# Attention and a dense mixture of experts on one core: padding TensorE's program early, joining local scores, re-cutting the last product

## The chip, the core and the metric
One core of one Trainium2 chip. Five engines run their own programs side by side: TensorE (PE: matrix products; its weight loads are listed as PEld), VectorE (DVE), ScalarE (ACT), GpSimd (POOL) and SyncE (SP, which here only asks for transfers). 16 DMA engines move data between main memory and the on-chip memory SBUF. Matrix products land in PSUM, a small memory of eight banks. The metric is the device time of one execution in microseconds (us), lower is better.

## The reference
```python
# q, k, v: 4 batches x 8 heads x 576 positions x 64, float32
scores = q @ k.T / 8
# heads 0..3 ("local"): position i sees j with 0 <= i - j < 32
# heads 4..7 ("strided"): i sees j <= i with i % 32 == j % 32
attn = exp(scores - max); attn = attn / (sum + 1e-9)
x = (attn @ v), heads side by side        # 2304 tokens x 512
p = probs / (probs.sum(-1) + 1e-9)        # 2304 x 4
out = sum over 4 experts e of p[:, e] * (relu(x @ w1[e]) @ w2[e])
# w1: 512 x 1024, w2: 1024 x 512
```

## The kernel before
**Work and tiles.** Attention is computed in 16 pairs (n = 0..15: a batch and a quarter of its heads, two heads of one kind), even n local (L), odd n strided (S). A pair's scores are many small products into PSUM banks of the pool "sc" (L616 for a strided pair, L627 for a local pair; a local pair's nine tiles go in two groups, gi = 0 with six and gi = 1 with three). VectorE masks them into `pmL`/`pmS` (L641) and takes the maximum, the sum and the quotient; PE transposes them (L706, L722, L739), and multiplies by the values `vstL`, `vstS` (L791 for early local pairs, L771). The result, x, is split into a rounded part `xh` (ACT, L849) and the rest `xl` (DVE, L852).

**Experts.** The first 384 tokens (of batch 0, whose four pairs are the first four) go through the experts in ordinary products of three passes (high x high, high x low, low x high): L969 for the first layer, L985 for the second. Its four chunks need the x of one pair each. The other 1920 tokens run in two parts of 896 and 1024 with a scheme of seven products per block step (`product`, L1155); there an operand is either a weight block reloaded into `a`, `s` (L1180), or a block from a ring of five buffers (`ring`, L1395), both brought by SP from main memory. A part has eight units, a unit 14 steps of 12 products or so.

**Order.** Nothing is ordered by hand. Each operation is given to a planner (class `Plan`) with an engine, a duration, the names that it reads and writes, a priority and the PSUM banks that it takes. Operations are numbered as they are added, and the table `SHIFT` moves single numbers' priorities. The planner walks a model of time and writes each engine's program. PSUM pools are "mo" (4 banks), "sc" (2) and "ps" (2). Into gaps that it foresees on PE in the first part it puts dummies (L1526): products of a tile `wz` of zeros, 128x512, whose result nobody reads.

**Engine queues.** Each engine runs its program in order, so that what stands behind a waiting instruction waits too, SP's transfers among them.

**Names.** `raw` are weights as loaded (L874), which ACT (L884) and DVE or POOL (L885) split into a high and a low part in `a`, `s`, `w2t` or `ring`. `normalize` (L1462) turns the expert probabilities into `pr`. At the end, the last product of the last unit is made in two column halves, each followed by an add (L1338) and a store (L1340).

Of the kernel before, what the change touches and what calls it, by code (L numbers as in the profile page):

```python
# [18 lines left out]
ZN = 30  # L19
# [10 lines left out]

SHIFT = {
# [5 lines left out]
}  # L37


# [4 lines left out]
class Plan:  # L44
# [14 lines left out]
    DEEPER = 5.0  # L59
    ROW = 1.0  # L60
    SWITCH = 0.17
    FIRST = 9
    SWING = 5.09
    ENGINES = ("PE", "ACT", "DVE", "POOL", "SP")
    FLEX = {"VP": ("DVE", "POOL"), "AD": ("ACT", "DVE")}
# [76 lines left out]
    def walk(self):  # L142
# [32 lines left out]
        def fill(f, s, o):  # L175

            n = 0
            while True:
                k = int(f / self.TICK + 1e-9)
                need = self.BUSY - seen.get(k, 0)  # L180
                rate = 1.0 if warm(f) else 0.5
                step = 0.2133 / rate
                if need <= 0:
                    nk = (k + 1) * self.TICK
                    if nk + step < s:
                        f = nk
                        continue
                    return n, f
                rem = (k + 1) * self.TICK - f
                forced = f > 3.4 and need / 2400 / rate <= rem and (  # L190
                    need - o.cols) / 2400 / rate > rem - max(s - f, 0.0) - o.dur / rate
                if f + step > s and not forced or not out and n >= self.FIRST:
                    return n, f
                f = stream(f, 0.2133, 512)
                n += 1
# [6 lines left out]
        def when(o):  # L202
            t = o.ready
            if o.xfer is not None and o.start is None:
                t = max(t, wire - (self.DEEP if wire < 200 else self.DEEPER))
            for i, key in enumerate(o.bank):
                n = len(allocs[key[0]]) - self.banks[key[0]] + i
                if n >= 0:
                    for p in self.readers.get(allocs[key[0]][n], ()):
                        if p.start is None:  # L210
                            return None
                        t = max(t, p.end + self.SYNC)
            return t
# [81 lines left out]
        while left:  # L295
# [29 lines left out]
            if e == "PE":  # L325
                f = free["PE"]
                if o.moe:
                    credit = min(credit + o.dur, 8.0)
                    began = True
                else:  # L330
                    credit = max(credit - o.dur * self.mix, -8.0)
                row = 0.0 if o.moe else row + o.dur
                if abs(credit) > self.swing:
                    turn = credit < 0
                if row > self.ROW:
                    turn = True
                if s < STEADY:
                    f = max(f, 1.07)
                    tag = next((t for t in allocs if not (o.bank and o.bank[0][0] == t) and clear(t, f) and not (began and t == "mo")), None)
                    n, f2 = fill(f, s, o) if tag else (0, f)  # L340
                    if n:
                        out.append((f, -1, n, tag))
                        allocs[tag].append(("idle",))
                        s = max(s, f2)
# [46 lines left out]
def attn_moe_kernel(  # L391
# [51 lines left out]
    psums = const.tile([P, NTT], F32, name="psums")  # L443
    wz = const.tile([P, 512], BF16, name="wz")
    warm = const.tile([P, 8], F32, name="warm")

    wt = {n: big.tile([P, 2, 2, 256], F32R, name=n) for n in QUART[:3] + ("s3",)}
    wq = {n: (t[:, 0], t[:, 1]) for n, t in wt.items()}
# [41 lines left out]
    KORD = (0, 2, 1, 3)  # L490
    JOIN = 4
    WHOLE = (1,)
    order = [(b, c) for b in range(B) for c in KORD]
    NP = len(order)
    plan = Plan(BANKS, MIX, tc)
# [44 lines left out]
    def plan_pair(n):  # L540
# [56 lines left out]
        for gi, (g0, g1) in enumerate(GRP[kd]):  # L597
            z = zg[gi]
            ng = g1 - g0
            key = ("sc", n, "b", gi)  # L600
            nel = ng * W

            keys = [key]
# [5 lines left out]
            def scores(keys=keys, gi=gi, g0=g0, g1=g1, v0=0):  # L609
                ss = [bank(x) for x in keys]  # L610
                if kd == "S":
                    for o in range(0, 6 * W, W):
                        for x in range(2):
                            for h in range(2):
                                a = slice(64 * h, 64 * h + 64)
                                nc.tensor.matmul(  # L616
                                    ss[h][64 * x:64 * x + 64, o:o + W], qkv[a, x, o:o + 64],
                                    qkv[a, x, QKS + o:QKS + o + SR], start=True, stop=True)
                    return
                for r in range(3):  # L620
                    for v, s in enumerate(ss, v0):
                        for h in range(2):
                            for i in range(2):
                                a = slice(64 * h, 64 * h + 64)
                                t = QB * (2 * gi + v) + (96 * i + 32 * r if spans else 64 * r + 32 * i)
                                p = 64 * (h ^ v) + 32 * i
                                nc.tensor.matmul(  # L627
                                    s[p:p + 32, r * W:r * W + W], qkv[a, t:t + 32],
                                    qkv[a, t + 193:t + 193 + W], start=True, stop=True)
# [33 lines left out]
            dd = nel / 960 + 0.15  # L663
            vp = (dd, nel * 1.6e-3 + 0.22)
            if kd == "S" and gi == 0:
                add("PE", 0.88, scores, [f"qkS{bf}{i}" for i in range(2)], keys + [f"pmS{bf}{i}" for i in range(2)], z + 3, keys,
                    cols=4 * nel)
            elif n == 0 and gi == 0:
                for i, x in enumerate(keys):
                    add("PE", 0.46, half_scores(scores, x, i), [f"qkL{bf}0" + "ab"[i]], [x, tok], z + 3, x, cols=2 * nel)  # L670
            elif kd == "L":
                add("PE", (0.68, 0.46)[gi], scores, [f"qkL{bf}{gi}"], keys + [tok], z + 3, keys, cols=4 * nel)
            for i, x in enumerate(keys if kd == "L" else [key]):
# [102 lines left out]
        for gi in range(2):  # L776
# [65 lines left out]
            for (t0, nt, nm) in ((0, TA, "x"), (T0[1], TBS[0], "r1"), (T0[2], TBS[1], "r2")):  # L842
                for sel, cols in cut(t0, nt):
# [3 lines left out]
                    if nm == "x":  # L847
# [5 lines left out]
                                out=cols(xl[c]), in0=src(), in1=cols(xh[c].bitcast(F32)), op=ALU.subtract)  # L853

                        add("ACT", 0.42, xhi, [key], [f"xh{c}{g}"], z + 7.2)
                        add("DVE", 0.44, xlo, [key, f"xh{c}{g}"], [f"xl{c}{g}"], z + 7.4)
                    else:
                        def xraw(e, src=src, cols=cols, nm=nm):
                            if e == "ACT":
# [454 lines left out]
    def plan_o(part, u, step, slot, group, last, z, due):  # L1314
# [10 lines left out]
        for f in range(2):  # L1325
# [6 lines left out]
            o0 = t0 + c * TH  # L1332
            orow = slice((2 * r + f) * P, (2 * r + f) * P + P)
            if last and step == "a22" and f == 1:
                for x in range(2):
                    cs = slice(x * TH // 2, (x + 1) * TH // 2)
                    add("PE", 0.72, lambda cs=cs, key=key: product(lhs(), rhs(), 1, key, first_in, TH, cs), need, [f"{key}{x}"], zz, None, True, 3 * TH)
                    add("DVE", 0.42, lambda i=i, cs=cs, key=key: nc.vector.tensor_tensor(  # L1338
                        out=acc[i][:, cs], in0=held[key][:, cs], in1=acc[i][:, cs], op=ALU.add), [f"{key}{x}", f"acc{i}0"], [f"end{x}"], zd)
                    add("SP", 0.4, lambda i=i, cs=cs, x=x, orow=orow, o0=o0: nc.sync.dma_start(  # L1340
                        out=out_t[orow, o0 + x * TH // 2:o0 + (x + 1) * TH // 2], in_=acc[i][:, cs]),
                        [f"end{x}"], [f"out{i}{x}"], zz + dz, xfer=((0.5, 128),))
                continue
            add("PE", dz, lambda f=f, key=key: product(lhs(), rhs(), f, key, first_in, TH),
# [116 lines left out]

    def normalize():  # L1462
        nc.vector.tensor_reduce(out=psums, in_=prs, op=ALU.add, axis=AX.X)
        nc.vector.tensor_scalar_add(out=psums, in0=psums, scalar1=1e-9)
        nc.vector.reciprocal(out=psums, in_=psums)
        nc.vector.tensor_tensor(
            out=pr, in0=prs, in1=psums.unsqueeze(2).to_broadcast([P, NTT, E]), op=ALU.mult)
# [5 lines left out]
        if n == 1:  # L1473
            add("POOL", 0.1, lambda: nc.gpsimd.memset(raws[2][:, 0, 0:1], 0.0), ["pmS00"], ["raw20", "raw21"], 0)
    add("SP", 0.4, load_pr, (), ["prs"], 8, xfer=((0.1, 128),))
    add("DVE", 1.0, normalize, ["prs"], ["pr"], ZN)
    key = ("ps", "pr")

    def turn_pr():
# [47 lines left out]

    with tc.manual_schedule():
        nc.vector.memset(wz, 0.0)
        make_identity(nc, ident)  # L1530
        for t in pm["S"]:
            nc.gpsimd.memset(t[:, :, SR + 1:64], 0.0)
            nc.gpsimd.memset(t[:, :, SR:SR + 1], 1e-9)
        for t in pm["L"]:
            nc.gpsimd.memset(t, 0.0)
            a = t[:, 0:1]
            nc.gpsimd.memset(bass.AP(a.tensor, a.offset, [list(a.ap[0]), [3 * P, 3], [P + 32, 3], [1, 1]]), 1e-9)
        plan.run(idle)
# [81 lines left out]
```

## Time and profile before

| what | value |
|---|---|
| median of 3 runs | 778.45 us (776.25, 778.45, 778.79) |
| profiled execution | 778.49 us, its span 776.7 |
| granted TensorE clock, mean | 0.998 |
| PE, DVE, ACT, POOL busy | 99%, 80%, 50%, 27% |
| first second-layer product (L985) | starts at 39.23 |
| last PE matmul ends | about 772.8 |

The span runs from the first to the last instruction; 1.8 us of the execution lie outside it. A time within the profile is counted from the start of the span. A matmul of 32-bit floats that the program writes once is shown as two instructions in rows of the trace (x24 in the program's order is x48 there). The granted clock is a share of the full 2.4 GHz; 0.5 is the lower level, 1.2 GHz.

### The profile page before, as it was taken

The page shows a single profiled execution, that of the slowest core. Times are in us where ns is not written, and L with a number is a line of the kernel's source. Part 1 is how long each engine was busy: PE and PEld are TensorE (multiplying, and loading weights), DVE is VectorE, ACT ScalarE, POOL GpSimd, SP SyncE. Part 2 cuts the span into 40 slices and gives each one's busy share as a digit, 9 for nine tenths or more (in the row PEclk, how much of TensorE's full clock was granted, in tenths as well). Part 3 has the DMA queues.
Part 4 walks back from the last instruction along what each step waited for, and adds up shares of the span by engine and source line. Part 5 has one row for each costly group of instructions (what it writes and reads, how often), then busy time and mean ns, then how long its engine had stood idle before and what let it go on. Part 6 is the DMA issues. An engine that isn't in the chain of part 4 may idle for free.

```text
span 776.7 us, 14119 instructions
## 1 busy us (share of the span) xinstructions
PE 765.5 (99%) x5374; PEld 664.6 (86%) x5377; DVE 620.8 (80%) x1016; ACT 385.6 (50%) x726; POOL 206.4 (27%) x198
## 2 busy tenths in 40 slices
PE   7999999999999999999999999999999999999997
PEld 4788888889989999999999998888888888888886
DVE  6877777798698897889798997758765976599895
ACT  4635544474566375646727654644354344523330
POOL 5412011012131522454373264001000330033250
PEclk9999999999999999999999999999999999999999
DMA  9999999778899798899989838955665697659624
GB/s 321 305 394 380 339 326 353 276 252 327 311 388 343 257 359 288 328 237 350 350 254 275 272 119 221 395 207 220 236 265 198 193 215 288 232 173 247 215 82 162
DMA packets 89630, 212.67 MB, mean 274 GB/s; under 512 B 7071, under 2 KB 33883, under 8 KB 89563
## 3 DMA queue, kind: packets, MB, share of 16 engines
q1 hardware_dynamic: 83659, 201.96, 71.8%
q0 software_dynamic: 5760, 9.70, 7.9%
q8 instruction: 42, 0.69, 0.3%
q10 hardware_dynamic: 144, 0.11, 0.1%
q14 instruction: 25, 0.20, 0.1%
HBM read 138.58 MB, written 73.17 MB: 273 GB/s over the span
## 4 chain that ended last, share of the span: by engine, by line
PE 95%; DVE 2%; DMA 1%; ACT 1%; issue 1%; POOL 0%; DVEq 0%; ACTq 0%
PE mo L1155 26%; PE ps L1155 25%; PE sc L1155 20%; PE mo L985 9%; PE mo L969 9%; PE ps L771 2%; DMA ring<-d27a 1%; PE sc L627 1%; PE ps L739 1%; PE sc L616 1%; PE mo L1526 1%; PE ps L791 0%; ACT q L1207 0%; DVE w2t L885 0%; DVE pmL L641 0%
## 5 line engine op out<-in xcount | busy, mean ns | idle before, releaser
L1155 PE MATMUL sc<-T,ring 128*128 128x448 f32 (+2 forms) x774 | 174.3, 374 | 0.0
L1155 PEld LDWEIGHTS sc<-T,ring 128*128 128x128 f32 x774 | 144.5, 188 | 19.7
L1240 ACT ACTIVATE T<-q 128x512 fp32r<-128x512 f32 (+1 forms) x196 | 112.6, 601 | 69.0 <-PE mo L1155 26.4
L1242 DVE TENSOR_TENSOR T<-q,T 128x512 fp32r<-128x512 f32 (+1 forms) x152 | 104.7, 703 | 15.9 <-ACT T L1240 15.2
L1203 DVE TENSOR_TENSOR q<-ps,v 128x448 f32<-128x448 f32 (+1 forms) x96 | 62.5, 654 | 35.3 <-PE ps L1155 30.9
L1155 PE MATMUL mo<-T,ring 128*128 128x512 f32 (+1 forms) x396 | 90.0, 376 | 0.0
L1207 ACT ACTIVATE q<-q 128x448 f32<-128x448 f32 (+1 forms) x84 | 49.9, 598 | 71.7 <-DVE q L1203 70.8
L1155 PEld LDWEIGHTS mo<-T,ring 128*128 128x128 f32 x396 | 74.3, 188 | 10.3
L1242 POOL TENSOR_TENSOR T<-q,T 128x448 fp32r<-128x448 f32 (+1 forms) x44 | 53.1, 1215 | 91.8 <-ACT T L1240 69.9
L985 PE MATMUL mo<-w2t,hs 128*128 128x512 f32 x288 | 71.2, 397 | 0.0
L1194 ACT ACTIVATE v<-mo 128x448 f32<-128x448 f32 (+1 forms) x96 | 54.5, 567 | 25.7 <-PE mo L1155 25.0
L1352 DVE TENSOR_TENSOR acc<-sc,acc 128x512 f32<-128x512 f32 (+1 forms) x85 | 54.9, 654 | 13.9 <-PE sc L1155 13.1
L1284 POOL TENSOR_TENSOR q<-q,q 128x512 f32<-128x512 f32 (+1 forms) x12 | 15.4, 1284 | 181.5 <-DVE T L1242 164.9
L985 PEld LDWEIGHTS mo<-w2t,hs 128*128 128x128 f32 x288 | 52.7, 188 | 11.0
L1284 DVE TENSOR_TENSOR q<-q,q 128x448 f32<-128x448 f32 (+1 forms) x88 | 58.9, 681 | 2.5 <-POOL T L1242 1.4
L526 ACT ACTIVATE acc<-sc 128x448 f32<-128x448 f32 (+1 forms) x41 | 23.2, 567 | 48.5 <-PE sc L1155 46.9
L969 PE MATMUL mo<-xh,a 128*128 128x384 f32 x192 | 45.7, 341 | 0.0
L1352 DVE TENSOR_TENSOR acc<-mo,acc 128x512 f32<-128x512 f32 (+1 forms) x52 | 34.0, 658 | 14.0 <-PE mo L1155 11.3
L1155 PE MATMUL ps<-T,ring 128*128 128x448 f32 (+1 forms) x180 | 40.8, 375 | 0.5 <-DMA ring<-d27a 0.5
L1155 PEld LDWEIGHTS ps<-T,ring 128*128 128x128 f32 x180 | 33.7, 188 | 5.3 <-DVE acc L1352 0.8
L1155 PE MATMUL ps<-t4h,a 128*128 128x448 f32 (+1 forms) x128 | 35.2, 376 | 0.2 <-DVE q L1203 0.2
L1155 PE MATMUL ps<-t3h,s 128*128 128x448 f32 (+1 forms) x128 | 35.2, 376 | 0.1
(179 smaller groups left out, 1437.6 us busy)
## 6 DMA issues: line engine op xcount, KB each, us to landing
raw<-in_w SPq DMA_DIRECT2D x28, 1024.0 KB, 8.3
qkS<-in_qk_strided SPq DMA_DIRECT2D x16, 329.0 KB, 8.2
vstL<-in_v_local SPq DMA_DIRECT2D x6, 640.0 KB, 9.7
po<-acc POOLq DMA_DIRECT2D x16, 224.0 KB, 7.2
vstS<-in_v_strided SPq DMA_DIRECT2D x8, 384.0 KB, 7.8
a<-d16a SPq DMA_DIRECT2D x6, 512.0 KB, 8.7
ring<-d27a SPq DMA_DIRECT2D x6, 512.0 KB, 6.5
a<-d10a SPq DMA_DIRECT2D x6, 512.0 KB, 4.7
```

The source lines that it names most:

```text
L526: nc.scalar.activation(out=dst(), in_=src(held[key]), func=AF.Copy)
L771: nc.tensor.matmul(oo[hf][64 * h:64 * h + 64, o:o + w], a, pt[r, x, c0:c0 + w], start=True, stop=True)
L969: nc.tensor.matmul(pt[:, 0:TA], w[:, c % 2, (f % 2) * P:(f % 2) * P + P], (xl if i == 1 else xh)[c], start=j == 0, stop=j == 11)
L985: nc.tensor.matmul(pt, ht[f][:, ts], wt[f][:, cs], start=j == 0, stop=j == 11)
L1155: nc.tensor.matmul(pt, a[i == 2][:, j, f * P:f * P + P], skewed(b[i == 1][j], TH)[:, cs], start=bool(first) and n == 0, stop=True, skip_gr ...
L1194: add("ACT", TH / 1200 + 0.18, lambda: nc.scalar.activation(out=late["u"][i][:, 0:TH], in_=held[key][:, 0:TH], func=AF.Copy), [key, "late2 ...
L1203: add("DVE", DD, lambda: nc.vector.tensor_tensor(out=q(), in0=src(), in1=late["u"][i][:, 0:TH], op=ALU.add), [key, f"u{i}", "late2"], [tok ...
L1207: add("ACT", TH / 1200 + 0.2, lambda: nc.scalar.activation(out=q(), in_=q(), func=AF.Relu), ["late2"], [tok], zs)
L1240: add("ACT", TH / 1200 + 0.17, lambda src=src, hi=hi: nc.scalar.activation(out=hi(), in_=src(), func=AF.Copy), [tok, "late2"], [f"T{i}h{j} ...
L1242: add("VP", vp, lambda e, src=src, hi=hi, lo=lo: engine(e).tensor_tensor(out=lo(), in0=src(), in1=hi().bitcast(F32), op=ALU.subtract), [to ...
L1284: add("VP", vp, lambda e, d=d, x=x, y=y: engine(e).tensor_tensor(out=d[0](), in0=x[0](), in1=y[0](), op=ALU.subtract), [x[1], y[1]], [d[1] ...
L1352: add("DVE", DD, lambda av=av, key=key: nc.vector.tensor_tensor(out=av(), in0=held[key][:, 0:TH], in1=av(), op=ALU.add), [key], tok, zd)
```

## The change
- The dummies ahead of PE's first operation are at most six (`FIRST`), not nine, counted until PE has run its first operation; foreseen gaps of up to 0.3 us (`SHORT`) get no dummies.
- Behind pair 1's scores stand twelve products of 128x64 zeros (`PAD`).
- From pair 4 on (`JOIN`) a local pair's scores are one operation, and its second group of three tiles takes a bank of "mo" instead of "sc". The count of banks in `when` is corrected for an operation that takes banks of two pools.
- `SHIFT` has new values, and the entries 814 to 842 are gone.
- The last product and its add and store are cut at 384 and 128 columns, not at 256 and 256.
- `normalize` adds 1e-9 from a tile `tiny` with a tensor_tensor; the planner's durations for it and for `xl` differ.

```diff
-    92: -3.6, 95: -12.5, 96: -7.9, 100: -3.6, 101: -23.3, 110: 14, 116: -12.2, 121: -23.9, 122: -23.9, 123: -42.2,
-    153: -19.6, 246: 21.6, 253: 14.6, 256: 14.6, 257: 14.6, 258: 14.6, 259: 14.6, 260: 14.6, 261: 14.6, 343: -7.1,
-    347: 2.4, 348: 6.9, 350: 17.1, 352: -6.9, 354: -22.2, 356: -12.9, 364: -31.5, 365: -12.6, 814: 2.4, 815: 6.9,
-    817: 17.1, 825: -22.2, 828: -6.9, 830: -12.9, 841: -31.5, 842: -12.6,
+    92: -3.6, 95: -12.5, 96: -7.9, 100: -3.6, 101: -23.3, 110: 14, 116: -12.2, 118: 5, 121: -23.9, 122: -23.9, 123: -42.2,
+    153: -19.6, 246: 21.6, 253: 14.6, 256: 14.6, 257: 14.6, 258: 14.6, 259: 14.6, 260: 14.6, 261: 14.6, 343: -7.1, 347: 2.4,
+    348: 6.9, 350: 17.1, 352: -6.9, 354: -22.2, 356: -12.9, 364: -31.5, 365: -12.6, 686: 7.8, 698: -5.2,
...
-    FIRST = 9
+    FIRST = 6
+    SHORT = 0.3
...
-                if f + step > s and not forced or not out and n >= self.FIRST:
+                if f + step > s and not forced or last["PE"] is None and n >= self.FIRST:
...
-                n = len(allocs[key[0]]) - self.banks[key[0]] + i
+                n = len(allocs[key[0]]) - self.banks[key[0]] + sum(x[0] == key[0] for x in o.bank[:i])
...
-                    n, f2 = fill(f, s, o) if tag else (0, f)
+                    n, f2 = fill(f, s, o) if tag and s - f > self.SHORT else (0, f)
...
+    tiny = const.tile([P, NTT], F32, name="tiny")
...
+    PAD = 12
...
-            key = ("sc", n, "b", gi)
+            whole = kd == "L" and n >= JOIN
+            key = ("mo" if whole and gi else "sc", n, "b", gi)
...
+                    for _ in range(PAD if n == 1 else 0):
+                        nc.tensor.matmul(ss[0][:, 6 * W:6 * W + 64], wz[:, 0:P], wz[:, 0:64], start=True, stop=True)
...
-                add("PE", 0.88, scores, [f"qkS{bf}{i}" for i in range(2)], keys + [f"pmS{bf}{i}" for i in range(2)], z + 3, keys,
-                    cols=4 * nel)
+                add("PE", 0.88 + (PAD * 0.03 if n == 1 else 0), scores, [f"qkS{bf}{i}" for i in range(2)], keys + [f"pmS{bf}{i}" for i in range(2)], z + 3, keys,
+                    cols=4 * nel + (PAD * 64 if n == 1 else 0))
             elif n == 0 and gi == 0:
                 for i, x in enumerate(keys):
                     add("PE", 0.46, half_scores(scores, x, i), [f"qkL{bf}0" + "ab"[i]], [x, tok], z + 3, x, cols=2 * nel)
+            elif whole:
+                if gi:
+                    plan.number += 1
+                else:
+                    k3 = keys + [("mo", n, "b", 1)]
+                    add("PE", 1.14, lambda scores=scores, k3=k3: (scores(), scores(k3[2:], 1)), [f"qkL{bf}{i}" for i in range(2)],
+                        k3 + [f"pmL{bf}{i}" for i in range(2)], z + 3, k3, cols=4 * 9 * W)
...
-                        add("DVE", 0.44, xlo, [key, f"xh{c}{g}"], [f"xl{c}{g}"], z + 7.4)
+                        add("DVE", 0.54, xlo, [key, f"xh{c}{g}"], [f"xl{c}{g}"], z + 7.4)
...
-                for x in range(2):
-                    cs = slice(x * TH // 2, (x + 1) * TH // 2)
-                    add("PE", 0.72, lambda cs=cs, key=key: product(lhs(), rhs(), 1, key, first_in, TH, cs), need, [f"{key}{x}"], zz, None, True, 3 * TH)
-                    add("DVE", 0.42, lambda i=i, cs=cs, key=key: nc.vector.tensor_tensor(
+                for x, (c0, c1) in enumerate(((0, 3 * TH // 4), (3 * TH // 4, TH))):
+                    cs = slice(c0, c1)
+                    add("PE", 6 * (c1 - c0 + 32) / 2400, lambda cs=cs, key=key: product(lhs(), rhs(), 1, key, first_in, TH, cs), need, [f"{key}{x}"], zz, None, True,
+                        6 * (c1 - c0))
+                    add("DVE", (c1 - c0) / 960 + 0.15, lambda i=i, cs=cs, key=key: nc.vector.tensor_tensor(
                         out=acc[i][:, cs], in0=held[key][:, cs], in1=acc[i][:, cs], op=ALU.add), [f"{key}{x}", f"acc{i}0"], [f"end{x}"], zd)
                     add("SP", 0.4, lambda i=i, cs=cs, x=x, orow=orow, o0=o0: nc.sync.dma_start(
-                        out=out_t[orow, o0 + x * TH // 2:o0 + (x + 1) * TH // 2], in_=acc[i][:, cs]),
+                        out=out_t[orow, o0 + cs.start:o0 + cs.stop], in_=acc[i][:, cs]),
...
-        nc.vector.tensor_scalar_add(out=psums, in0=psums, scalar1=1e-9)
+        nc.vector.tensor_tensor(out=psums, in0=psums, in1=tiny, op=ALU.add)
...
-    add("DVE", 1.0, normalize, ["prs"], ["pr"], ZN)
+    add("DVE", 0.85, normalize, ["prs"], ["pr"], ZN)
...
+        nc.vector.memset(tiny, 1e-9)
```

In the order rows below, `N<-a,b` is the output tile and the inputs (numbers tell buffers apart), then the shape, and x24 a count of equal rows. Lines of the changed kernel are some 12 higher: L627 is L632 there, L616 L619, L706 L718, L771 L783, L791 L803, L969 L981, L985 L997, L1180 L1192, L1395 L1408, L1526 L1539.

**PE at its start.** In the kernel before, PE's program opens with eight dummies, of which the last stands first here, and the first pair's scores come in halves with a dummy between.
```order
L1526 MATMUL mo<-wz 128x512
L627 MATMUL sc<-qkL_261 32x63 x12
L1526 LDWEIGHTS wz
L1526 MATMUL mo<-wz 128x512
L627 MATMUL sc<-qkL_261 32x63 x12
L627 MATMUL sc<-qkL_262 32x63 x24
L1526 LDWEIGHTS wz
L1526 MATMUL mo<-wz 128x512
L1526 LDWEIGHTS wz
L1526 MATMUL mo<-wz 128x512
```
In the changed kernel six dummies open the program, pair 0's first scores are one piece, and the last two of five later dummies open this piece; pair 1's scores follow, and the first two of the pad's twelve weight loads and products.
```order
L1539 MATMUL mo<-wz 128x512
L1539 LDWEIGHTS wz
L1539 MATMUL mo<-wz 128x512
L619 MATMUL sc<-qkS_264 64x54 x24
L623 LDWEIGHTS wz
L623 MATMUL sc<-wz 128x64
L623 LDWEIGHTS wz
L623 MATMUL sc<-wz 128x64
```
The pad's 24 instructions stand ahead of all that PE does later.

**PE around pair 1's value products.** The kernel before has the first group of pair 4's scores (L627) behind the L771 and three first-layer products.
```order
L969 MATMUL mo<-xh_242,s_80 128x384
L771 MATMUL ps<-pTS,vstS_267 64x54 x24
L969 MATMUL mo<-xh_242,s_80 128x384
L969 MATMUL mo<-xl_246,s_80 128x384
L969 MATMUL mo<-xh_242,s_80 128x384
L627 MATMUL sc<-qkL_261 32x63 x24
L791 MATMUL ps<-pTL,vstL_266 64x96 x8
L706 MATMUL ps<-ident,pmL_270 128x128 x3
L969 MATMUL mo<-xh_244,a_78 128x384
```
In the changed kernel the L803 (pair 2) follows at once, with two dummies behind it.
```order
L981 MATMUL mo<-xh_243,s_81 128x384
L783 MATMUL ps<-pTS,vstS_268 64x54 x24
L981 MATMUL mo<-xh_243,s_81 128x384
L981 MATMUL mo<-xl_247,s_81 128x384
L981 MATMUL mo<-xh_243,s_81 128x384
L803 MATMUL ps<-pTL,vstL_267 64x96 x8
L1539 LDWEIGHTS wz
L1539 MATMUL sc<-wz 128x512
L1539 LDWEIGHTS wz
L1539 MATMUL sc<-wz 128x512
L718 MATMUL ps<-ident,pmL_271 128x128 x3
L981 MATMUL mo<-xh_245,a_79 128x384
```
Pair 4's scores have moved from here to the place right ahead of the first second-layer product.

**SP in the second part.** A place in the second part, behind the load of `pb`. In the kernel before, the ring loads begin right there.
```order
L1381 DMA pb_2952<-dp 128x8x128
L1395 DMA ring_2947<-d20a_147 128x1024
L1180 DMA s_2591<-d11s_104 128x1024
L1395 DMA ring_2948<-d20s_150 128x1024
L1180 DMA s_2590<-d11s_102 128x1024
L1395 DMA ring_2949<-d20s_151 128x1024
L1180 DMA a_78<-d12a_106 128x1024
L1395 DMA ring_2950<-d20s_153 128x1024
```
In the changed kernel two reloads of `s` come first.
```order
L1394 DMA pb_2974<-dp 128x8x128
L1192 DMA s_2614<-d11s_105 128x1024
L1192 DMA s_2613<-d11s_103 128x1024
L1408 DMA ring_2969<-d20a_148 128x1024
L1192 DMA a_79<-d12a_107 128x1024
L1408 DMA ring_2970<-d20s_151 128x1024
L1192 DMA s_81<-d11s_104 128x1024
L1408 DMA ring_2971<-d20s_152 128x1024
L1192 DMA s_2612<-d12s_109 128x1024
```
Each ring load stands two reloads later than it did, and the same holds in the other units of this part.

## Rows read from the trace of the kernel before

**Rows 1.** The page: section 1, busy us and instructions; section 4, chain
```profile
PE 765.5 (99%) x5374; PEld 664.6 (86%) x5377; DVE 620.8 (80%) x1016; ACT 385.6 (50%) x726; POOL 206.4 (27%) x198
...
PE 95%; DVE 2%; DMA 1%; ACT 1%; issue 1%; POOL 0%; DVEq 0%; ACTq 0%
```

**Rows 2.** Waits of PE: what waited, for what, us in total, times, longest
```profile
PE ps L771 <- issue: 1.4, 1, 1.4
...
PE mo L969 <- DVE xl L852: 0.5, 1, 0.5
...
PE ps L1155 <- DMA ring<-d27a: 0.5, 1, 0.5
```

**Rows 3.** PE timeline, 13 to 27 us: start, us, what, [idle before <-releaser]
```profile
13.62 0.88 PE L791 MATMUL ps<-pTL,vstL 128*64 128x96 f32 x16 [0.79 <-ACT pmS L651]
...
15.40 0.59 PE L1526 MATMUL mo<-wz 128*128 128x512 bf16 x2
...
20.98 0.78 PE L771 MATMUL ps<-pTS,vstS 54*64 54x54 f32 x34
23.14 0.45 PE L771 MATMUL ps<-pTS,vstS 54*64 54x54 f32 x14 [1.38 <-issue]
...
25.58 1.54 PE L791 MATMUL ps<-pTL,vstL 128*64 128x96 f32 x16
```

**Rows 4.** A window: busy us (instructions) by engine, granted clock, DMA share, GB/s
```profile
23.70:27.10 3.40, 3.40 (x68) 2.57 (x68) 2.27 (x6) 1.59 (x4) 0.86 (x3) 0.51 1.06 375
```

**Rows 5.** PE timeline, 32 to 40 us
```profile
32.75 0.44 PE L969 MATMUL mo<-xh,s 128*128 128x384 f32 x1
...
34.00 0.72 PE L627 MATMUL sc<-qkL 64*32 64x63 f32 x48
...
36.16 0.44 PE L969 MATMUL mo<-xl,a 128*128 128x384 f32 x1 [0.52 <-DVE xl L852]
...
38.38 0.92 PE L616 MATMUL sc<-qkS 64*64 64x54 f32 x48
39.23 0.51 PE L985 MATMUL mo<-w2t,hs 128*128 128x512 f32 x1
```

**Rows 6.** DMA queues from 20 to 22.3 us: packets, MB, share
```profile
q8 instruction: 1, 0.02, 4.5%
```

**Rows 7.** The page, section 3: the same queue over the whole span
```profile
q8 instruction: 42, 0.69, 0.3%
```

**Rows 8.** DMA issues at 6.0, 22.1, 221.7 and 630.0: KB, us to landing
```profile
vstL<-in_v_first SPq DMA_DIRECT2D x1, 384.0 KB, 7.5
...
raw<-in_w SPq DMA_DIRECT2D x1, 1024.0 KB, 8.3
...
ring<-d27a SPq DMA_DIRECT2D x1, 512.0 KB, 9.8
...
ring<-d22a SPq DMA_DIRECT2D x1, 512.0 KB, 10.4
```

**Rows 9.** PE timeline at 120 us, 24 small matmuls between two large ones
```profile
120.69 0.53 PE L627 MATMUL sc<-qkL 64*32 64x63 f32 x24
```

**Rows 10.** VectorE timeline, 29 to 36 us
```profile
29.44 1.10 DVE L1464 TENSOR_SCALAR psums<-psums 128x18 f32<-128x18 f32 x1
...
34.43 1.21 DVE L885 TENSOR_TENSOR a<-raw,a 128x512 fp32r<-128x512 f32 x1
35.56 0.54 DVE L852 TENSOR_TENSOR xl<-ps,xh 128x216 fp32r<-128x216 f32 x1
```

**Rows 11.** Timelines of SP, PE and VectorE, second part and end
```profile
629.99 0.57 SPq L1395 DMA_DIRECT2D ring<-d22a  x1
...
644.70 2.88 PE L1155 MATMUL sc<-T,ring 128*128 128x512 f32 x12
647.42 2.88 PE L1155 MATMUL mo<-T,ring 128*128 128x512 f32 x12
...
772.80 0.76 DVE L1338 TENSOR_TENSOR acc<-sc,acc 128x256 f32<-128x256 f32 x2 [0.74 <-PE sc L1155]
```

## The prediction
> **What bounds the kernel now.** I read three views in this order. The page first: 95% of the chain that ended last is PE [rows 1], so only what stops or slows PE counts. The waits of PE second: they are few, and the dearest is one of 1.4 us ahead of an L771, with nothing named that released it ("issue"); the others that this change can touch are an L969 that waits for xl (0.5) and an L1155 that waits for a ring load (0.5) [rows 2]. PE's timeline third: the 1.4 us cut pair 1's L771 in two, 34 instructions ahead and 14 behind, at 21.76 to 23.14 [rows 3]. In the window view the granted clock behind that pause, from 23.7 to 27.1, is 0.51, the lower of the two levels; PE is busy in all 3.40 us of it, at half speed [rows 4]. So the pause costs twice, and both costs lie in the first 27 us. Behind the first second-layer product (39.23 [rows 5]) the ring's wait is the only one of half a microsecond.
>
> **What the pause is.** No semaphore ended it. One 16 KB packet of an instruction queue, q8, moved just then [rows 6], and the page has 42 of them for the 5374 matmuls and 5377 weight loads of PE [rows 1, 7], 10751 instructions, one per 256. I read it as PE's program running dry: the block of instructions behind row 34 of that L771 had not arrived, while the DMA engines were full of loads (share 1.06 right behind it [rows 4]). The Trainium skill ("Runtime: NRT & Kernel Launch", section "Instruction fetch mechanics") agrees that blocks are 16 KiB, 256 instructions, but says that crossing into the next is mostly hidden since the engine's own queue fetches ahead; by that the 1.38 us would be something else and pads could not move it. The row shows one crossing in 42 that is not hidden; the other side is the first rival below.
>
> **Edits, with what they cost**
> - *Pads.* Twelve matmuls with twelve weight loads put 24 instructions ahead of everything from pair 1's transposes on. The old dry point, the end of a block, then falls 24 instructions earlier: 45 into that L771 where it was 69 (matmuls and weight loads counted). It also makes PE pass the place where the fetch is asked for ahead of the L791 that stands waiting until 13.62 [rows 3], not behind it, so the block is asked for up to 2 us sooner. The pause of 1.38 us therefore shrinks to between 0 and 0.6; I take 0.3: **-1.1**. The pads themselves (64 columns each, shorter than any row shown; bound 0 to 0.3 us each, from the 0.59 of two 512-column dummies [rows 3]) stand ahead of that same L791, which waits for a v load asked for at 6.02 and landed 7.5 later, 13.5 [rows 8]: whatever they take up to about a microsecond is hidden there. Without that cover they would cost what they last.
> - *Half clock.* It followed the pause; a pause of 0.3 should not bring it. L791 x16 lasted 1.54 in it against 0.88 at 13.62 [rows 3], 43% lost; that share of all 3.40 us [rows 4] is 1.46, the L791 alone 0.66. I take a value near the first, as all matmuls of the window ran at that clock: **-1.3**.
> - *Six dummies, whole first scores, short gaps unfilled.* Everything ahead of 13.5 waits there for the v load [rows 8]; earlier first scores are lost. 0 (bounds -0.1 and +0.1). If that load were early they would be worth up to the two dummies' 0.5.
> - *Local scores in one operation.* Pair 4's scores leave their place behind L771 and now stand, with the second group, ahead of the first second-layer product; in the old place go two dummies, whose pair lasted 0.59 with an end that overlaps what follows [rows 3]: **+0.45**. Ahead of 39.23 two groups disappear and come later: the L616 at 38.38 (0.85 to the next start, so 0.07 of its 0.92 overlaps) and the L627 at 34.00 (0.72 less 0.07, 0.65) [rows 5]: **-1.5** there. Later they must run: +1.5, less the saving that three groups of scores run in one piece. By the rows, 48 instructions take 0.72 and 24 take 0.53 [rows 5, 9], so a piece of its own costs 0.17 over its share. By the order there are two separated groups fewer (0.2 each, an estimate from that 0.17) and four pieces fewer (0.1 to 0.17): **+0.7** (bounds -0.3 and +1.1).
> - *xl of the third chunk.* Its product waits 0.52 now [rows 2, 5]. It is fed by the L771 ahead: that ends at 32.75, where the next product starts [rows 5], and the last xl starts at 35.56 and lasts 0.54 [rows 10], 3.35 us behind it. Without its 0.52 PE is at this place at 35.64 now; less 1.1 and 1.3, less the three groups of scores that stood ahead (0.65, 0.46, 0.65: 48, 24 and 48 instructions [rows 5, 9] less the overlap) and plus 0.45, it comes at 31.9. The L783 (the old L771) ends at 32.75 less all of these but the last 0.65: 29.7. And 29.7 + 3.35 is 33.05, a wait of 1.15. VectorE has an `a` product from a weight load between the two xl halves in both orders; that load is asked for at 22.12 and takes 8.3 [rows 8], landing at 30.4, which bounds the chain from below: 30.4 plus the product (1.21) and an xl (0.54) is 32.2, a wait of 0.3. Upper bound 1.8, if load and chain add up in part. I take 1.5, toward that bound, since the product starts only when ScalarE has made its half of the weights, which no bound here counts: **+1.0**. The shorter normalize helps here: its 1.10 us TENSOR_SCALAR [rows 10] stands in the same VectorE queue; that it becomes 0.3 I count at nothing, since the load and not VectorE sets the lower bound.
> - *Sum to the first second-layer product*: -1.1 - 1.3 + 0.45 - 1.5 + 1.0 = -2.45; it starts near 36.8, not 39.23.
> - *SHIFT, ring load at 221.7.* That load is asked for with 9.8 us to landing [rows 8], and PE waits 0.5 [rows 2]. By the order it is asked for ahead of the pb load now: **-0.5** (0 to -0.5).
> - *SHIFT, second part.* The ring loads move behind two reloads of `s` or `a`, each of which waits for the end of a step; steps are 2.72 us apart [rows 11], so the loads are asked for 5.4 us later. In the tightest unit the first was asked for at 629.99, landed 10.4 later [rows 8], at 640.4, and was used at 647.42 [rows 11]: 7.0 to spare, 1.6 after. 0, as long as landing stays under 12.0.
> - *Last product 384 and 128 columns.* Both adds wait for the whole product now (0.74 of idle ahead of L1338, whose two adds take 0.76 [rows 11]), and so they do after. The first add grows by half a 256-column add (0.13), the second shrinks, narrow matmuls repay little: **+0.2** (0 to +0.3).
> - *Later blocks.* All later crossings move as well, 24 and more instructions, and two now fall where little work lies between the asking and the end. One short pause of 0 to 1.4; chance weighed: **+0.2**.
>
> Sum: -2.45 + 0.7 - 0.5 + 0.2 + 0.2 = -1.85. The profiled execution took 778.49 (span 776.7 and 1.8 around it), the median of the runs is 778.45: **776.6**.
>
> **Rivals**
> - *The pause stays, or another block runs dry.* For it: the DMA engines are as full at 9 to 27 us as they were, and the fetch can wait behind them. (By the section of the Trainium skill cited above, "Runtime: NRT & Kernel Launch", the pause would stay just where it is.) Against: the asking moves ahead of a wait that is 0.79 long [rows 3]. The 1.1 and the 1.3 are lost, and the xl wait of 1.0 extra isn't incurred since PE comes later, and the 0.2 goes: 776.6 + 2.4 - 1.0 = 778.0 at one end, 779.0 if PE waits for xl anyway. I take 778.6.
> - *The saving is taken by xl and the weight loads.* PE gains time only to wait for the load that lands at 30.4 and for ACT and VectorE that are full. The wait is 1.8 and not 1.5, later groups cost the full 1.1 and not 0.7, and a second, like wait of 0.6 follows at the next chunk: 777.9.
> - *Every wait goes.* The pause entirely (-0.3), xl at 0.52 as before (-1.0), no later pause (-0.2): 775.1.
> - *Slower: the ring loads of the second part come too late.* In a busy unit a load took 10.4 us [rows 8], and 1.6 us are left. It decides from the point where the landing passes 12.0: where one needs 13.2, PE waits 1.2 us, and the loads behind it follow 2.72 apart, no later than PE needs them. Four units with one such wait each give 776.6 + 4.8 = 781.4. Against: the pb load that it shared the queue with has landed before it is asked for.
>
> **How the numbers follow.** Forecast 0.45 (own range 775.6 to 777.6), pause stays 0.16, xl takes it 0.15, every wait goes 0.15, ring late 0.09. 0.3% of the median, 2.3 us, is about what a measurement can tell from no change: faster means under 776.1. A third of the forecast (0.15), all of "every wait goes" (0.15) and a little of the rest lie there: 0.34. Slower means over 780.8: the ring case and little more, 0.09. Same: 0.57. The range leaves out half of the 0.15 at the low end and the ring case at the top: 774.9 to 779.3.
>
> **What would show it.** After: no wait of over 0.6 with "issue" in the first 40 us, no window at half clock, the wait of L981 for xl near 1.5, first L997 near 36.8; no 0.5 us ring wait near 231; in the second part no PE idle over 0.2; the last store about 0.2 later behind the last matmul. Wrong, if the issue wait is found at another instruction or if the first L997 comes early and the gain is gone by 200 us.

## The result, and the profile after

| | before | changed |
|---|---|---|
| median of 6 runs each | 777.34 us | 782.11 us |
| lowest to highest | 776.21 to 778.79 | 780.61 to 782.84 |
| ratio, 95% interval | | 1.0058 [1.0042, 1.0075] |
| profiled execution, span | 778.49, 776.7 | 782.20, 778.7 |

The change made the kernel 0.58% slower. Outside the span lie 3.5 us in the changed kernel's profiled execution and 1.7 to 2.0 in its five others, so the trace shows less of the loss than the medians do. The profiled execution of before was a long one as well: taken again, its span is 774.6 (last experiment).

The page of the changed kernel still says PE [rows 1], with 2.3 us more of busy time for 26 more instructions:

```profile
PE 767.8 (99%) x5386; PEld 664.2 (85%) x5391; DVE 621.3 (80%) x1015; ACT 384.0 (49%) x725; POOL 209.6 (27%) x201
...
PE 97%; DVE 1%; ACT 1%; issue 0%; POOL 0%; DVEq 0%; ACTq 0%
```

The window that was at half clock [rows 4] is at full clock now. PE's waits (us in total, times, longest) show no stop of 1.4 us with "issue" any more [rows 2], but several shorter ones in its place; those of L783 and L632 add up to 2.1:

```profile
PE ps L783 <- issue: 1.4, 3, 0.5
...
PE ps L803 <- DVE xl L864: 0.9, 2, 0.7
...
PE sc L632 <- issue: 0.7, 1, 0.7
...
PE mo L981 <- DVE xl L864: 0.4, 1, 0.4
```
```profile
23.70:27.10 3.40, 3.24 (x32) 2.66 (x28) 3.33 (x7) 3.08 (x7) 2.74 (x5) 1.00 0.89 223
```

PE's timeline at the places of [rows 3, 5, 11], at the stops, and at steps of the two parts:

```profile
8.96 0.52 PE L623 MATMUL sc<-wz 128*128 128x64 bf16 x12
...
12.24 0.30 PE L632 MATMUL sc<-qkL 64*32 64x63 f32 x4 [0.70 <-issue]
...
20.98 0.61 PE L783 MATMUL ps<-pTS,vstS 54*64 54x54 f32 x25 [0.50 <-issue]
...
29.15 0.92 PE L783 MATMUL ps<-pTS,vstS 54*64 54x54 f32 x48 [0.48 <-issue]
...
32.97 0.44 PE L981 MATMUL mo<-xl,a 128*128 128x384 f32 x1 [0.35 <-DVE xl L864]
...
36.20 4.19 PE L997 MATMUL mo<-w2t,hs 128*128 128x512 f32 x17
...
243.40 0.57 PE L1167 MATMUL ps<-t3h,s 128*128 128x448 f32 x2
...
245.85 0.56 PE L1167 MATMUL mo<-t1h,s 128*128 128x448 f32 x2
...
645.32 2.88 PE L1167 MATMUL sc<-T,ring 128*128 128x512 f32 x12
648.04 2.88 PE L1167 MATMUL mo<-T,ring 128*128 128x512 f32 x12
...
664.36 0.63 PE L1167 MATMUL ps<-b11h,a 128*128 128x512 f32 x2
...
667.16 0.63 PE L1167 MATMUL mo<-b22h,s 128*128 128x512 f32 x2
...
669.91 0.61 PE L1167 MATMUL ps<-t2h,s 128*128 128x512 f32 x2
...
771.58 3.21 PE L1167 MATMUL sc<-T,ring 128*128 128x512 f32 x18
```

The first second-layer product starts 3.0 us earlier than in [rows 5], and yet the last matmul ends 2.0 later (774.8). PE hardly idles in between, so what got longer is the products themselves. A ring step takes 2.72 us as in [rows 11] (645.32 to 648.04); the b11 step, the same twelve products with other tiles, takes 2.80 (664.36 to 667.16), the b22 step 2.75. In the first part the t3 step takes 2.45 (243.40 to 245.85) where 2.40 is usual (below). Of a unit's seven steps that load weights into `a` or `s`, four have weights in the tiles a11, a12, a22 and s3, and these are the slow ones: 4 x 8 units x 0.05 in the first part and 4 x 8 x 0.08 in the second, with 2 x 8 x 0.03 for two of the other three (b22 and t1) in the second part, is 4.6 us.

Those four tiles are among those allocated behind the constants. The diff adds one there, `tiny`: 18 floats, which take 96 bytes of each partition once rounded up. Everything allocated behind it moved by 96 bytes; the products' right-hand operands (b11 to t4) and the tiles s1, s2, s4 are allocated from the other end and did not move.

### The profile page after: what moved, and what is told of

Read it like the earlier page. It is cut to its first block, busy times and chain, and to the rows that moved or that the text cites. A ratio compares the mean times of both kernels' runs of the same rounds, so it can differ in the third digit from the quotient of the medians.

```text
span 778.7 us, 14171 instructions
## 1 busy us (share of the span) xinstructions
PE 767.8 (99%) x5386; PEld 664.2 (85%) x5391; DVE 621.3 (80%) x1015; ACT 384.0 (49%) x725; POOL 209.6 (27%) x201
## 4 chain that ended last, share of the span: by engine, by line
PE 97%; DVE 1%; ACT 1%; issue 0%; POOL 0%; DVEq 0%; ACTq 0%
PE mo L1167 27%; PE ps L1167 26%; PE sc L1167 21%; PE mo L997 9%; PE mo L981 9%; PE ps L783 2%; PE ps L751 1%; PE sc L619 1%; PE sc L632 1%; PE mo L1539 0%; PE ps L803 0%; PE mo L632 0%; ACT q L1219 0%; PE ps L718 0%; POOL pmS L652 0%
## 5 line engine op out<-in xcount | busy, mean ns | idle before, releaser
L1215 DVE TENSOR_TENSOR q<-ps,v 128x448 f32<-128x448 f32 (+1 forms) x96 | 62.3, 654 | 36.8 <-PE ps L1167 32.6
L997 PE MATMUL mo<-w2t,hs 128*128 128x512 f32 x288 | 71.0, 397 | 0.0
L997 PEld LDWEIGHTS mo<-w2t,hs 128*128 128x128 f32 x288 | 52.8, 188 | 11.4
L981 PE MATMUL mo<-xh,a 128*128 128x384 f32 x192 | 45.6, 341 | 0.1
```

What stands on the lines that cost most here:

```text
L981: nc.tensor.matmul(pt[:, 0:TA], w[:, c % 2, (f % 2) * P:(f % 2) * P + P], (xl if i == 1 else xh)[c], start=j == 0, stop=j == 11)
L997: nc.tensor.matmul(pt, ht[f][:, ts], wt[f][:, cs], start=j == 0, stop=j == 11)
L1215: add("DVE", DD, lambda: nc.vector.tensor_tensor(out=q(), in0=src(), in1=late["u"][i][:, 0:TH], op=ALU.add), [key, f"u{i}", "late2"], [tok ...
```

## Experiments

In what follows theory P is this: the tile moved weights against right-hand operands, and products of such pairs slowed. Theory O: the new order slowed them. Theory B, on the early stage: the profiled execution of before was a costly one, so there was less to gain there than the rows said. "Before" is run beside each kernel on the same chip; its median was 776.58, 776.63 and 776.93 in the three groups of runs.

**The changed kernel without the tile**
```diff
-    tiny = const.tile([P, NTT], F32, name="tiny")
...
-        nc.vector.tensor_tensor(out=psums, in0=psums, in1=tiny, op=ALU.add)
+        nc.vector.tensor_scalar_add(out=psums, in0=psums, scalar1=1e-9)
...
-        nc.vector.memset(tiny, 1e-9)
```


> The changed kernel with the tile of 18 floats gone and the scalar add of before back in its place; every engine's order is that of the changed kernel. Theory P (placement): the tile moved all tiles behind it by 96 bytes, and each product whose weights moved while its right-hand operand did not became 2% slower, 4.7 us in all. It expects matmul starts 0.2000 and 0.2267 us apart again, no idle added, 782.1 - 4.7 = 777.4. Theory O (order): the new order makes products slower through other traffic. It expects 782.1 within 0.8, and starts 0.2044 and 0.2340 apart.


777.30 (12 runs), ratio to before 1.0007 [0.9998, 1.0016]; steps at 2.40 and 2.72 again. The loss is gone, and with it nothing that could be called a gain is left. Theory O falls.

**The kernel before with only the tile**
```diff
     warm = const.tile([P, 8], F32, name="warm")
+    tiny = const.tile([P, NTT], F32, name="tiny")
...
+        nc.vector.memset(tiny, 1e-9)
```


> The kernel before with only the tile of 18 floats added, set once and never read. Theory P: 777.3 + 4.7 = 782.0, with starts 0.2044 and 0.2340 apart where weights of a11, a12, a22 or s3 are used. Theory O: 777.3 within 0.8, starts 0.2000 and 0.2267 apart.


781.43, ratio 1.0060 [1.0047, 1.0073]. An unread tile costs as much as the whole change. By form, 520 to 700 us (count, busy us, mean ns of one), the products on `ring` keep their 389 ns and those of t3, whose weights are in s3, have 396:
```profile
L1156 PE MATMUL mo<-T,ring 128*128 128x512 f32 x120 | 28.8, 389 | 0.0
L1156 PE MATMUL ps<-t3h,s 128*128 128x512 f32 x40 | 11.8, 396 | 0.0
...
L1156 PE MATMUL mo<-b22h,s 128*128 128x512 f32 x32 | 9.3, 391 | 0.0
```
`T` and `ring` moved together; t3 and s3 did not. That is what theory P says.

**What it is about the place.** Four shifts, all read in the same rows.
```diff
 # the changed kernel: 128 bytes in all
     tiny = const.tile([P, NTT], F32, name="tiny")
+    const.tile([P, 8], F32, name="spare")
```


> The changed kernel with the tile kept and 32 bytes more beside it, so that the same tiles stand 128 bytes from their place before and not 96. If what counts is the distance between weights and right-hand operand modulo 64 bytes (theory P, first form): 777.4, paces as before. If any displacement from the tuned place costs (second form): 782. Theory O: 782.


781.45, ratio 1.0056 [1.0044, 1.0068]: as slow. A period of 64 bytes, the first form of theory P, is wrong.
```diff
 # before: left 32 bytes up, right-hand operands 32 bytes down
+    const.tile([P, 8], F32, name="spare")
...
-        p.tile([P, 16], F32, name="skew1")
+        p.tile([P, 24], F32, name="skew1")
```


> The kernel before with 32 bytes more on the left, so that weights start at a multiple of 64 bytes as in the changed kernel, and the right-hand operands moved 32 bytes too. If the distance counts: 777.3, paces 0.2000 and 0.2267 as before. If the weights' own place counts: 782, slow where the weights are on the left. Theory O: 777.3.


781.31, ratio 1.0055 [1.0043, 1.0067], t3 at 395 ns. I had called this the kernel that keeps the distance; it does not, since one end went up and the other down: weights and right-hand operands came 64 bytes nearer. It told nothing of the two forms apart, so the next one was made.
```diff
 # before: both 32 bytes up
+    const.tile([P, 8], F32, name="spare")
...
-        p.tile([P, 16], F32, name="skew1")
+        p.tile([P, 8], F32, name="skew1")
```


> The kernel before with 32 bytes more on the left and a filler on the right 32 bytes shorter, so that weights and right-hand operands all stand 32 bytes higher and their distance stays what it was. If the distance between the two counts (theory D): starts 0.2000 and 0.2267 us apart, 776.6. If a tile's own place counts (theory A): weights at a multiple of 64 bytes as in the slow kernels, 781.


776.75, ratio 1.0000 [0.9991, 1.0009]. The weights that slowed stand here where they stood in the kernel before this one (32 bytes up in both), which was slow; only the right-hand operands, with the other tiles of their end, stand elsewhere. And in the changed kernel the right-hand operands had not moved, and the products slowed. So neither place alone decides: the distance between the two does.
```diff
 # before: left 256 bytes up
+    const.tile([P, 64], F32, name="spare")
```


> The kernel before with 256 bytes more on the left alone. In it the distance between the fast pairs of tiles is a multiple of 256 bytes, or 64 more; in the slow kernels, which were moved by 64 to 128, it is not. If the distance counts with a period of 256 bytes: 776.6, starts 0.2000 and 0.2267 apart. If every move from the tuned place costs, or the period is longer: 781.


776.70, ratio 1.0000 [0.9991, 1.0008]; the same rows read
```profile
L1156 PE MATMUL mo<-T,ring 128*128 128x512 f32 x120 | 28.8, 389 | 0.0
...
L1156 PE MATMUL ps<-t3h,s 128*128 128x512 f32 x40 | 11.5, 389 | 0.0
```
Distances changed by 0 and 256 bytes are fast, by 64, 96 and 128 slow. If the rule is periodic, its period is 256 bytes: any smaller power of two would have made the change of 128 a fast one. But no single distance is the fast one for every product. In the first part, with 448 columns, the right-hand operands start 64 bytes further into their tiles (`skewed`). The second kernel of these four (64 bytes nearer) therefore gives its first part just the distance that t3 and s3 have in the second part of before, where they are fast. Its t3 step takes 2.43 all the same (243.39 to 245.82), not 2.40:
```profile
243.39 0.57 PE L1156 MATMUL ps<-t3h,s 128*128 128x448 f32 x2
...
245.82 0.56 PE L1156 MATMUL mo<-t1h,s 128*128 128x448 f32 x2
```
So the expectation above, that fast pairs are a multiple of 256 bytes apart or 64 more, is not a rule that holds in both parts.

**The pads alone**
```diff
+    PAD = 12
...
+                    for _ in range(PAD if n == 1 else 0):
+                        nc.tensor.matmul(ss[0][:, 6 * W:6 * W + 64], wz[:, 0:P], wz[:, 0:64], start=True, stop=True)
```


> The kernel before with the twelve small matmuls and nothing else of the change; the rest of the order is the same. By the prediction's terms the pads take 1.1 of pause and 1.3 of half clock: 774.2. Theory B: the profiled execution of before was a costly one; other executions have a shorter pause and no half clock (two kernels with the order of before and other places showed 0.8 to 1.0 and a clock of 1.00), so the pads give at most half a microsecond: 776.0 to 776.8.


778.23 (776.41 to 780.55), ratio 1.0018 [1.0009, 1.0027]: they cost 1.4 us, which neither theory gave. The trace is of the slowest of the eleven runs (780.55); which stops a typical run has isn't shown. In this one PE stops four times with "issue":
```profile
12.99 0.30 PE L630 MATMUL sc<-qkL 64*32 64x63 f32 x4 [0.94 <-issue]
...
22.11 0.61 PE L774 MATMUL ps<-pTS,vstS 54*64 54x54 f32 x26 [0.98 <-issue]
...
33.93 0.55 PE L794 MATMUL ps<-pTL,vstL 128*64 128x96 f32 x7 [0.71 <-issue]
...
78.75 0.30 PE L630 MATMUL sc<-qkL 64*32 64x63 f32 x4 [1.58 <-issue]
```
The last stop is followed by 3.7 us near the lower clock, 0.54 (in the form of [rows 4]):
```profile
79.40:83.10 3.70, 3.70 (x15) 3.70 (x14) 2.51 (x5) 1.03 (x2) 0.00 (x0) 0.54 0.89 348
```
Counted in the program, each small product of 32-bit floats as four instructions (two matmuls with their weight loads), a transpose as two, and PE's waiting instructions with them, the stops lie near instructions 448, 704, 1216 and 2496, each 192 more than a multiple of 256. From 75 to 78 us one packet of the instruction queue moves:
```profile
q8 instruction: 1, 0.02, 2.0%
```
So the pads did not shorten the pause in L774 (the unchanged kernel's is 0.78, below), and they put other block ends where small matmuls crowd. The one at 12.99 lies ahead of an L794 that waited for a v load anyway; those at 33.93 and 78.75 don't: between 71.5 and 79 us stand 48, 72, 48 and 24 of them among twelve large ones.

**The changed kernel without tile and without pads** (`PAD = 0` in the first of these experiments)

> The changed kernel without the tile and without the twelve small matmuls (one dummy more, which the planner adds). By the prediction's terms the pause and the half clock come back: 777.3 + 2.4 = 779.7. Theory B: 777.3 within 0.8, since a pause of some tenths in L783 is there with the pads too and the half clock is rare.


776.33 (776.11 to 776.80), ratio 0.9996 [0.9987, 1.0005]. The prediction's 779.7 is missed, and theory B's lower bound by 0.2: it had the pads cost nothing. By the two ratios to before (1.0007 with pads, on another chip) they cost some 0.9 in the new order, with intervals that overlap, and the runs spread over 0.7 us where they spread over 3.4 with pads. One pause came at another place:
```profile
60.94 0.30 PE L631 MATMUL mo<-qkL 64*32 64x63 f32 x4 [0.80 <-issue]
```

**A version with all of this put right**
```diff
-    tiny = const.tile([P, NTT], F32, name="tiny")
+    tiny = const.tile([P, 64], F32, name="tiny")[:, 0:NTT]
-    PAD = 12
+    PAD = 0
...
-                for x, (c0, c1) in enumerate(((0, 3 * TH // 4), (3 * TH // 4, TH))):
+                for x, (c0, c1) in enumerate(((0, TH // 2), (TH // 2, TH))):
...
+        calls.append(n)
-        for _ in range(n):
+        for _ in range(n - 2 if len(calls) == 3 else n):
```


> The changed kernel with the tile in a slot of 256 bytes (so the distances of before are kept), no pads, two of the early dummies left out (four instructions fewer, so that the block end that fell on a dense place at 60 us falls later), and the last product cut at 256 and 256 columns. If placement and the position of block ends were what cost: 776.3 of the kernel without tile and pads, less the pause of 0.8 at 60 us, less 0.26 of the last product: 775.3, with no pause named issue over 0.7. If other parts of the new order cost as well, they stay: 776.3 or more.


776.78, ratio 0.9998 [0.9989, 1.0007]: a miss. The tile in a slot of 256 bytes costs nothing, as expected. But the pause at 60 us is still there, 0.81 long at 60.8, and one of 0.9 stands in L783. The four instructions left out moved the block end by just four instructions, two rows further in the same group (2 rows are left behind it, 4 before), so the aim of getting it out of the dense place was missed. The last product is 2.95 long again:
```profile
61.61 0.27 PE L632 MATMUL mo<-qkL 64*32 64x63 f32 x2 [0.81 <-issue]
...
768.43 2.95 PE L1167 MATMUL sc<-T,ring 128*128 128x512 f32 x18
```
No kernel here beats the one before by more than a measurement can tell.

**The kernel before, once more**

> The kernel before, unchanged, profiled once more. If the profile that the prediction rested on was a costly execution (theory B): the pause in L771 near 0.8, no window at half clock, first L985 near 36.7, last matmul near 770.3. If it was typical: 1.4, 0.51 in 23.7 to 27.1, 39.2 and 772.8.


776.38. Its timeline and window:
```profile
21.90 0.45 PE L771 MATMUL ps<-pTS,vstS 54*64 54x54 f32 x14 [0.78 <-issue]
...
36.84 6.45 PE L985 MATMUL mo<-w2t,hs 128*128 128x512 f32 x27
...
244.11 0.56 PE L1155 MATMUL ps<-t3h,s 128*128 128x448 f32 x2
...
246.51 0.56 PE L1155 MATMUL mo<-t1h,s 128*128 128x448 f32 x2
```
```profile
23.70:27.10 3.40, 2.97 (x32) 2.54 (x30) 3.31 (x10) 2.96 (x6) 1.22 (x4) 1.00 0.93 231
```
The pause is 0.78, not 1.38 [rows 3]; there is no half clock [rows 4]; the first L985 starts at 36.84, not 39.23 [rows 5]. The two kernels whose tiles were moved harmlessly show the same (pauses of 0.8, a clock of 1.00, 36.7 and 36.8). The two slow kernels of this order have 0.29 and 0.83 in L771, and full clock. So in six traces of this order the pause is 1.38 in one, with half a clock behind it, and 0.29 to 0.83 in the others: theory B holds for the profiled execution. How often such a costly one comes isn't known: of the 71 times of before on record four are above 778.1, three of them among the six beside the changed kernel, and none of these four has a trace.

## Why the prediction was wrong

**The step that failed most is that of normalize.** It counts the new add "at nothing" and looks at VectorE alone; that the add brings a tile, and the tile an allocation, is not in the sum. The tile's 96 bytes are the whole loss: +4.9 alone (781.43 against 776.58), and without it the changed kernel is at 1.0007. Without the tile, 777.30 lies inside the range that was given, but by luck: the forecast of 776.6 is where the kernel before usually stands (776.58 to 776.93 in three groups), and the gains that led there from 778.45 are mostly missing, as said below. No rival had the tile either. The one on the slower side, late ring loads, came near the measured time by another road, and its mechanism was not seen: in the tightest unit the ring load was asked for at 634.72, 4.7 us later than in [rows 11] where 5.4 was forecast, landed 9.1 us later, at 643.8, and was used at 648.04.

**The term of the pause and the half clock, -2.4, was mis-sized for the kernel's usual execution.** Reading the pause as the end of an instruction block fits every trace: the stops with "issue" inside a group of small matmuls sit multiples of 256 instructions apart, and the 24 instructions of the pads moved the one in pair 1's value products from behind row 34 to behind row 23, as forecast. That the next block had not arrived is inferred from this and from the moving packets. But the rows of one execution made it 1.38 and half a clock; the repeated profile says 0.78 and full clock. So 0.6 and 1.3 of the 2.4 were there in one of the six traced executions of that order, and of the pause that stays, 0.5 is left in L783. A new stop of 0.70 stands in L632 at 12.24, which is what the prediction named as a sign of being wrong: an issue wait at another instruction. The rule of the Trainium skill ("Runtime: NRT & Kernel Launch", "Instruction fetch mechanics"), that crossings are mostly hidden, agrees with the traces for most of the 42, and not for the one to four stops in each kernel here.

**"Later blocks" was mis-sized the other way**: forecast +0.2 with pads that gain 1.1; measured, the pads alone cost 1.4. In the slowest execution of that kernel one later block end took 1.58 and was followed by the slow clock, the pair of costs that the pads were to remove at L771.

**Early stage.** The first L997 was forecast at 36.8 and started at 36.20. The xl wait at the third chunk was 0.35, not 1.5; two waits of L803 for xl (0.9 in sum) came in its place, and a pause of 0.48 ahead of the second L783. That pause is no block end: it stands ahead of the same group with and without pads. PE starts 0.1 behind the end of a VectorE copy to its operand `pTS`, and this copy stood in VectorE's queue right behind normalize, whose last product took 0.97:
```profile
27.61 0.97 DVE L1479 TENSOR_TENSOR pr<-prs,psums 128x72 f32<-128x72 f32 x1
28.50 0.55 DVE L530 COPY pTS<-ps 128x384 f32<-128x384 f32 x1
```
In the kernel before ScalarE makes both copies of this pair, and nothing waits there; the prediction's sum has no such wait. Against 36.84 in the repeated profile of before this is 0.6 earlier with 1.5 us of work put off: no gain that shows, and without tile and pads the ratio of 0.9996 shows none over the whole kernel.

**Small terms.** The ring wait at 231 was forecast to go, and did; but in seven traces with SP's order of before the wait is 0.7, 0.5, 0.4 and 0.4, and three of them list none, so this was a gain of 0.7 at most. The last product is 3.21 us long against 2.95 with equal halves, +0.26 for +0.2. Normalize saved nothing: its add from a tile took 1.00 us on VectorE, against 1.10 for the scalar one [rows 10], which takes 1.00 in the repeated profile.

## What to carry to other kernels

Before costing an edit by its instructions, list every tile that it allocates and compare the addresses of all tiles behind it; where one end of the memory moves and the other does not, look at products that take an operand from each. Profile the kernel before a second time before a term of the sum rests on a pause of a single execution. And instructions added early move each later block end: look where the next ones fall, not only at the one that is to go.

## What the runs showed of the hardware

- The pace of a product depends on the distance in bytes between its weights and its right-hand operand within a partition. With 512 columns a step of twelve took 2.72 us at the distances of before and 2.80 with the two 96 bytes nearer; a change of 256 or 0 left it alone. Why, the traces don't show: weight loads last 0.188 us in both. Nor is it shown why steps whose two tiles had not moved (b22 with s4, t1 with s1) took 2.75 in the second part, and were not slowed in the first; both follow right on a slowed step, while t2, which follows b22, kept its 2.72.
- PE stops in the midst of small matmuls, 0.3 to 1.6 us each time, at places a multiple of 256 instructions apart, with the DMA engines busy (a share of 0.75 to 1.06 around the stops that were looked at). The same stop differs between executions of one order, 0.29 to 1.38 in L771. The two longest, 1.38 and 1.58, were followed by 3.4 and 3.7 us at a granted clock of 0.51 and 0.54; behind stops of 0.78, 1.04 and 1.15 it was 1.00.
